# An attention and mixture-of-experts kernel: padding rows as indirect scatters, a drain behind them, and two subtractions on another engine

## The chip, the cores and the metric

The kernel runs on one core of a Trainium2 chip. The metric is device time in microseconds (us), the median of several runs. A core has five engines, each with an instruction stream of its own, which it works through in order: TensorE (PE: matrix products), VectorE (DVE), ScalarE (ACT), GpSimd (POOL) and SyncE (SP, which here only issues DMAs). They wait for each other, and for DMAs, through semaphores. Sixteen DMA engines move the data that SP and GpSimd ask for.

## The reference

First comes attention with random features: for each batch and head, `q` and `k` are projected on 128 random directions, exponentiated, and combined without a softmax over keys. Its output, one row of 512 values for each of 4608 tokens, is the input `x` of a mixture of 8 experts with one expert per token:

```
q_p, k_p = phi(q * scale), phi(k * scale)          # phi: projection on omega, exp
num = q_p @ (k_p^T v);  den = q_p . sum(k_p) + 1e-6
x = (num / den) as [4608, 512]

logits = normalized(x) @ normalized(expert_emb)^T / tau
expert_idx = argmax(logits, axis=1);  gate_w = softmax(logits)[expert_idx]
for e in range(8):
    mask = expert_idx == e
    h = maximum(x[mask] @ w1[e], 0)                # 512 -> 1024
    out[mask] = gate_w[mask] * (h @ w2[e])         # 1024 -> 512
```

## The kernel before

**First stage.** A loop works on 36 tiles of 128 tokens. For each tile it forms the features, the attention output and the logits; for each three tiles it chooses the experts and counts tokens (`routed`). GpSimd then writes each tile's 128 rows (512 values, 8 logits and the token's number: 521 floats) into a DRAM tensor `xs` with one indirect DMA (L592). There each expert has a region of 4736 rows, and a token's row is the region's start plus the number of its expert's tokens so far. Beside the last tiles TensorE already computes steps 0 and 1 of the second stage (`first_steps`).

**Second stage.** It has 38 steps of 128 rows of one expert each; step `t` begins with a load of 128 rows of `xs` on SP's queue (`xload`, L189). TensorE turns the rows (L269), multiplies with `w1`, and then with `w2` (L287). Every float32 value is split into a high and a low part, so each product takes three matmuls. The result is written to the rows of `y` that the token numbers name, by an indirect DMA of GpSimd (`store`, L317); a row whose number is too large is skipped.

**Weights.** Each step also loads a quarter of the `w1` and of the `w2` of an expert to come (`wload`, L205) and splits it (`wsplit`). For the first four quarters ScalarE makes the high part (L232), and VectorE (`w1`) or GpSimd (`w2`) subtracts it from the loaded value for the low part (L234).

**Padding.** The last step of an expert reads up to 127 rows behind its last token. These must hold a token number that `store` skips. So when all tiles are routed, 128 rows of padding are written behind each expert's last row, from `padrow`, an SBUF tile. The first row's place comes from `runi`, which VectorE computes (L985 to L989). `pad(0)`, for the expert of steps 0 to 2, is issued on SP. The seven others are ordinary DMAs of GpSimd (L993); GpSimd loads each place from `runi` into a register first (L992), and in front of all seven stands a drain (L998), at which GpSimd stops until its earlier work is done.

**What sets the order.** All engines are written out by hand here (`manual_schedule`): an engine's order is the order of the code. Waits come from what each instruction reads and writes, corrected by `declare_no_dep` and `add_manual_dep`. `xload` lets step 3 (`NPRE + 1`) go without the seven last paddings, while step 4 waits for all of them. The pools `p1`, `small` and `once` end with the first stage (`c1`, L325), and the pool `p2` (L1073) takes their memory; the `xs` rows of steps 3 and 4 (`xg`) lie in `p2`. GpSimd's DMAs use eight semaphores in turn, named DMASW0 to DMASW7.

Of the kernel before, what the change touches and what calls it, by code (L numbers as in the profile page):

```python
# [13 lines left out]
I32 = mybir.dt.int32  # L14
# [3 lines left out]
ALU = mybir.AluOpType  # L18
AX = mybir.AxisListType
ET = mybir.EngineType  # L20
PSUM = bass.MemoryType.PSUM

P = 128
B, H, S, D, M = 8, 8, 576, 64, 128
E, F = 8, 1024
# [7 lines left out]
GPICK = 5  # L33
DUM = E * REG
ROWS = DUM + P
RS = 576
PAY = DM + E + 1
NQ = 4
LAG = 7
NPRE = 2  # L40
# [1 line left out]
LOADS = {29: 0, 30: 2, 31: 1, 33: 4, 35: 6, 36: 3, 37: 5, 39: 7}  # L42
LOADS_LATE = 33
FILLS = {36: 1, 37: 1, 38: 1, 39: 1, 40: 1, 41: 1, 42: 2, 43: 4, 44: 5}
PADP = 8
ONACT = 3
DRAINS = (4,)
KPROJ = {0: (0,), 1: (1, 2), 2: (3,), 3: (4,), 4: (5,), 5: (6,)}
# [14 lines left out]
WHY = "computed on the chip from counts that sum to the token number"  # L63
# [3 lines left out]
def attention_moe(ctx: ExitStack, tc: tile.TileContext, qT, kT, v1, omT, emb, tau, w1q, w2q, xs, out):  # L67
    nc = tc.nc
# [39 lines left out]
    stepf = const.tile([P, 1], F32, name="stepf")  # L108
# [15 lines left out]
    runi = const.tile([P, E], I32, name="runi")  # L124
# [10 lines left out]
    put, got, outs, last_x, junks, kept = [], [], [], [], [], {}  # L135
# [4 lines left out]
    padrow = w1l[:, 1, 2, 0:PAY].bitcast(F32)  # L140
# [41 lines left out]
    def written(w):  # L182

        for o in put + got:
            tc.declare_no_dep(w.ins, o.ins.name, reason="other rows")
        put.append(w)

    def xload(t, row, xg):
        r = nc.sync.dma_start(xg, xs[ds(row, P), 0:PAY])  # L189
        if t in range(NPRE + 3):  # L190
            for j, w in enumerate(put):
                if t < NPRE and j > 3 * GPICK + 3 and w is not kept.get(t) or t == NPRE + 1 and j > len(put) - PADP:

                    tc.declare_no_dep(r.ins, w.ins.name, reason="other rows")
                else:
                    tc.add_manual_dep(r.ins, w.ins.name, sync, reason="rows written in any order")
        else:
            tc.add_manual_dep(r.ins, last_x[0].ins.name, sync, reason="behind an earlier step's wait")
        got.append(r)
        last_x[:] = [r]  # L200
        return xg
# [25 lines left out]
    def wsplit(wn, t, raw, dv, dp):  # L227
        _, h, l = W[wn]
        at = lambda a, d: a.rearrange("p a q f -> p (a q) f")[:, ds(d, 1), :].rearrange("p o f -> p (o f)")
        if t is not None and t < NQ:  # L230

            ih = nc.scalar.activation(h[:, 1, t, :], raw, AF.Copy)  # L232
            eng = nc.vector if wn == "w1" else nc.gpsimd
            ils = [eng.tensor_tensor(l[:, 1, t, :], raw, h[:, 1, t, :].bitcast(F32), op=ALU.subtract)]  # L234
        else:
            ih = nc.vector.tensor_copy(at(h, dv), raw)  # L236
            ils = []
            piece = F if t is None or t >= NSTAT - 2 else PIECE
            eng, d = (nc.vector, dv) if wn == "w2" and t is not None and t >= NSTAT - 2 else (nc.gpsimd, dp)
            for c in range(0, F, piece):  # L240
                c = slice(c, c + piece)
                ils.append(eng.tensor_tensor(at(l, d)[:, c], raw[:, c], at(h, d)[:, c].bitcast(F32), op=ALU.subtract))  # L242
        if t is None:
            return
        for w in (ih, *ils):
            seq[w] = len(seq)
            if t >= NQ:
                tc.add_manual_dep(w.ins, mmi[wn, t - 1][-1].ins.name, sync, reason="the buffer's last use")
        for o in range(NSTAT):
            apart(wn, (ih, *ils), t, mmi.get((wn, o), ()), o)  # L250
        if t < NPRE:

            for w in put:
                for il in ils:
                    tc.declare_no_dep(il.ins, w.ins.name, reason="another part of the weights")
        for w in spl.get((wn, t - 1), ())[1:]:
            tc.declare_no_dep(ih.ins, w.ins.name, reason="another part of the weights")
        spl[wn, t] = (ih, *ils)
# [3 lines left out]
    def flush():  # L262
        while lows:
            lows.pop(0)()
# [60 lines left out]
    with ExitStack() as c1:  # L325
# [453 lines left out]
        for i in range(NTILE + LAG + 2):  # L779
# [15 lines left out]
            if i == XLOAD:  # L795
                prow = [nc.values_load(
                    firsti[0:1, t : t + 1], engines=[ET.SP], min_val=t * P, max_val=(E - 1) * REG + t * P,
                    skip_runtime_bounds_check_because=WHY) for t in range(NPRE + 1)]
# [183 lines left out]
        vt = nc.vector  # L982
        t = lambda n, w=E, dt=F32: once.tile([P, w], dt, name=n)
# [3 lines left out]
        vt.tensor_copy(runi[:, 0:1], swp[:, 0:1])  # L987
        vt.tensor_scalar(swp[:, 1:2], run[:, 0:1], swp[:, 0:1], None, op0=ALU.subtract)
        vt.scalar_tensor_tensor(runi[:, 1:], isf[:, 1:], swp[:, 1:2], run[:, 1:], op0=ALU.mult, op1=ALU.add)  # L989
        def pad(e):  # L990
            eng, et = (nc.gpsimd, ET.Pool) if 0 < e < PADP else (nc.sync, ET.SP)
            v = nc.values_load(runi[0:1, e : e + 1], engines=[et], min_val=0, max_val=DUM - P, skip_runtime_bounds_check_because=WHY)  # L992
            written(eng.dma_start(xs[ds(v, P), 0:PAY], padrow))  # L993

        pad(0)
        xload(NPRE, prow[NPRE], xgp[NPRE])

        nc.gpsimd.drain()  # L998
        for e in range(1, PADP):
            pad(e)  # L1000


        row = lambda a: a.unsqueeze(1).to_broadcast([P, E, E])
# [52 lines left out]
        vt.tensor_scalar(r, tab[:, 1:2], -float(NQ), float(NQ), op0=ALU.mult, op1=ALU.add)  # L1056
        vt.tensor_tensor(tab[:, 3:4], r, q4, op=ALU.add)
        vt.tensor_copy(tab[:, 4:5], total)
        for _ in range(FILL2):
            next(fill, None)  # L1060
            flush()
# [88 lines left out]
    with tc.manual_schedule(engines={ET.PE, ET.Activation, ET.DVE, ET.Pool, ET.SP}):  # L1150
# [82 lines left out]
        for t in range(NPRE, NSTAT):  # L1233
# [11 lines left out]
            if early:  # L1245
                wn = joined(t - 1)
# [43 lines left out]
            if late and not early:  # L1290
                wn = words(t - 1), turn[t - 1][0].shape[1] * P
# [134 lines left out]
```

## Time and profile before

| what | value |
|---|---|
| median of 3 runs | 630.5 us (629.82 to 630.67) |
| the profiled execution | 630.09 us |
| its span, first to last instruction | 628.4 us |
| TensorE (PE) busy | 620.4 us, 99% |
| VectorE (DVE) busy | 496.5 us, 79% |
| ScalarE (ACT) busy | 432.5 us, 69% |
| GpSimd (POOL) busy | 421.2 us, 67% |
| mean granted TensorE clock | 0.998 of full speed |

The profiled execution took 1.7 us more than its span, for what lies around the first and the last instruction. Busy time is the time in which an engine had an instruction in work. Starts of instructions are counted from the start of the span. The name of a tile before an arrow is what is written, behind it what is read. A name at an idle time ("<-") is what ended last before the engine went on. The DMA rows of a queue give the time of the issue; the transfer lands later.

### The profile page before, as it was taken

The numbers are of one execution on the slowest core, as the hardware profiler recorded it, in microseconds if no ns is written. First come the engines' busy times: TensorE is split into PE (matmuls) and PEld (weight loads), VectorE is DVE, ScalarE is ACT, GpSimd is POOL, SyncE is SP. The second block draws the span as 40 slices with busy tenths as digits, with TensorE's granted clock in tenths as the row PEclk, the third lists the DMA queues.
The fourth block names the chain that finished last, engine by engine and source line by source line (L and its number), as shares of the span: only waits on it lengthen the run. The fifth ranks groups of instructions, "written<-read, shape, count | busy, mean of one in ns | idle before, by whom it ended". The sixth has DMA issues, their size and how long they took to land.

```text
span 628.4 us, 19172 instructions
## 1 busy us (share of the span) xinstructions
PE 620.4 (99%) x6337; PEld 531.1 (85%) x6338; DVE 496.5 (79%) x917; ACT 432.5 (69%) x1135; POOL 421.2 (67%) x603
## 2 busy tenths in 40 slices
PE   9999999999999999999999999999999999999996
PEld 8999999999988787888888888888888888888885
DVE  5799899898989836779787877887887886877764
ACT  6999899899888237675757566656666656575630
POOL 3013344456887534588898878896987989796862
PEclk9999999999999999999999999999999999999999
DMA  7754776777772487698787796867787775968731
GB/s 259 221 154 156 240 198 206 223 220 237 274 254 79 154 305 253 187 273 233 225 217 238 180 263 189 244 191 211 226 211 243 201 245 171 255 196 197 221 118 47
DMA packets 143263, 132.19 MB, mean 210 GB/s; under 512 B 107766, under 2 KB 107894, under 8 KB 143168
## 3 DMA queue, kind: packets, MB, share of 16 engines
q1 hardware_dynamic: 136544, 109.96, 60.7%
q0 software_dynamic: 6480, 20.91, 8.6%
q8 instruction: 57, 0.93, 0.6%
q14 instruction: 38, 0.31, 0.2%
q10 hardware_dynamic: 144, 0.07, 0.0%
HBM read 83.78 MB, written 21.97 MB: 168 GB/s over the span
## 4 chain that ended last, share of the span: by engine, by line
PE 89%; issue 3%; DVE 3%; POOL 1%; ACT 1%; DMA 1%; POOLq 1%; DVEq 0%; ACTq 0%
PE po L287 30%; PE pb L287 30%; PE pb L376 11%; PE kva L408 5%; PE nuu L485 5%; PE nuu L465 2%; PE fs_a L287 1%; PE nuu L408 1%; DMA raww<-w2q 1%; DVE nmq L380 1%; PE pb L94 1%; POOLq L992 0%; PE pb L435 0%; DMA qt<-qT 0%; POOL w2l L234 0%
## 5 line engine op out<-in xcount | busy, mean ns | idle before, releaser
L242 POOL TENSOR_TENSOR w2l<-raww,w2h 128x256 f32 x128 | 140.3, 1096 | 7.6
L242 POOL TENSOR_TENSOR w1l<-raww,w1h 128x256 f32 (+1 forms) x130 | 116.0, 892 | 14.5 <-DMA xgp<-xs 5.2
L287 PE MATMUL po<-w2h,hh 128*128 (+1 forms) x288 | 112.3, 390 | 0.0
L287 PE MATMUL po<-w2l,hh 128*128 (+1 forms) x288 | 112.1, 389 | 0.0
L287 PE MATMUL po<-w2h,hl 128*128 (+1 forms) x288 | 112.1, 389 | 0.0
L287 PE MATMUL pb<-w1h,xh 128*128 (+1 forms) x280 | 109.6, 391 | 0.3 <-ACT nuu L298 0.3
L287 PE MATMUL pb<-w1h,xl 128*128 (+1 forms) x280 | 109.2, 390 | 0.0
L287 PE MATMUL pb<-w1l,xh 128*128 (+1 forms) x280 | 109.0, 389 | 0.0
L1140 DVE COPY pl<-pb 128x512 uint16<-128x512 uint16 x68 | 46.8, 690 | 59.8 <-ACT pl L1136 59.1
L1136 ACT ACTIVATE pl<-pb 128x512 uint16<-128x512 uint16 x68 | 39.4, 582 | 67.9 <-PE pb L287 65.2
L390 ACT ACTIVATE ftq<-pb,nmq 128x128 f32<-128x128 f32 x288 | 80.1, 415 | 4.2 <-DVE nmq L380 4.2
L317 POOL DMA_INDIRECT y<-xgp,tail x36 | 44.6, 1239 | 54.0 <-DVE w1h L236 30.2
L390 ACT ACTIVATE ftk<-pb,nmk 128x128 f32<-128x128 f32 x272 | 75.9, 466 | 4.5 <-DVE nmk L380 4.5
L1158 DVE COPY wd<-t 128x1024 uint16<-128x1024 uint16 x68 | 65.1, 959 | 1.6 <-DMA t<-pl 1.5
L1174 ACT ACTIVATE hh<-wd 128x1024 fp32r<-128x1024 f32 x34 | 36.1, 1063 | 42.1 <-DVE wd L1158 37.1
L287 PEld LDWEIGHTS po<-w2h,hl 128*128 128x128 f32 x288 | 54.1, 188 | 11.4
L287 PEld LDWEIGHTS po<-w2h,hh 128*128 128x128 f32 x288 | 54.1, 188 | 11.1
L287 PEld LDWEIGHTS po<-w2l,hh 128*128 128x128 f32 x288 | 54.0, 187 | 11.1
L287 PEld LDWEIGHTS pb<-w1h,xh 128*128 128x128 f32 x280 | 52.5, 188 | 11.3 <-ACT w2h L232 0.7
L287 PEld LDWEIGHTS pb<-w1h,xl 128*128 128x128 f32 x280 | 52.5, 188 | 11.2 <-DVE xl L271 0.2
L287 PEld LDWEIGHTS pb<-w1l,xh 128*128 128x128 f32 x280 | 52.7, 188 | 10.8
L1178 DVE SCALAR_TENSOR_TENSOR hl<-wd,hh 128x1024 fp32r<-128x1024 f32 x34 | 54.7, 1610 | 2.9 <-ACT hh L1174 2.3
(351 smaller groups left out, 1250.0 us busy)
## 6 DMA issues: line engine op xcount, KB each, us to landing
raww<-w1q SPq DMA_DIRECT2D x38, 512.0 KB, 4.5
raww<-w2q SPq DMA_DIRECT2D x38, 512.0 KB, 4.8
qt<-qT SPq DMA_DIRECT2D x36, 256.0 KB, 3.1
kt<-kT SPq DMA_DIRECT2D x35, 256.0 KB, 3.6
xg<-xs SPq DMA_DIRECT2D x23, 260.5 KB, 2.8
xgp<-xs SPq DMA_DIRECT2D x15, 260.5 KB, 3.6
rf<-w1q SPq DMA_DIRECT2D x4, 512.0 KB
rf<-w2q SPq DMA_DIRECT2D x4, 512.0 KB, 3.9
```

The source lines that it names most:

```text
L242: ils.append(eng.tensor_tensor(at(l, d)[:, c], raw[:, c], at(h, d)[:, c].bitcast(F32), op=ALU.subtract))
L287: done.append(nc.tensor.matmul(dst, x[:, c * P : (c + 1) * P], ws.rearrange("p o f -> p (o f)"), start=(begin and i == 0 and k == 0), stop ...
L317: w = nc.gpsimd.indirect_dma_start(out=out, out_offset=bass.IndirectOffsetOnAxis(ap=(xg[:, DM:] if tail is None else tail)[:, E : E + 1].b ...
L376: nc.tensor.matmul(st["pj" + w, i, a][:, c, :], st[w, i][r, c, :], om[r, :], start=True, stop=True)
L390: nc.scalar.activation(ft[:, h, :], pj[:, h, :], AF.Exp, bias=nm[:, h : h + 1])
L408: nc.tensor.matmul(acc[c : c + 64, h, :], ft[:, h, c : c + 64], vt[:, 2 * h + a, :], start=begin and h == 0, stop=u == 4 + 4 * b and h == 3,)
L485: nc.tensor.matmul(pn[a][s * D : s * D + D, h, :], st["qp", i, s][:, 2 * h + a, :], kvs[sb, int(u > 4 - s)][:, 4 * a + h, :], start=True, ...
L1136: nc.scalar.activation(planes[1][:, o : o + 512], halved(src)[:, :, 1], AF.Copy)
L1140: nc.vector.tensor_copy(planes[0][:, o : o + 512], halved(src)[:, :, 0])
L1158: nc.vector.tensor_copy(to, src)
L1174: nc.scalar.activation(hh, wd[:, 0:F], AF.Relu)
L1178: nc.vector.scalar_tensor_tensor(hl, wd[:, 0:F], 0.0, hh.bitcast(F32), op0=ALU.max, op1=ALU.subtract)
```

## The change

The seven paddings become indirect scatters. VectorE computes a table `padi` of 128 rows by 8 experts: the row of `xs` for each of the 128 padding rows, or a row beyond the end of `xs` for those that lie past the expert's last step, and these the DMA skips. The table lies in the pool `once`. The scatters need no registers. They and the drain now stand behind the code of the step table, with the drain behind the scatters; on GpSimd itself nothing else lay between. In `wsplit`, the low parts of `w2`'s quarters 0 and 1 move from GpSimd to VectorE.

```diff
-PADP = 8
...
-                if t < NPRE and j > 3 * GPICK + 3 and w is not kept.get(t) or t == NPRE + 1 and j > len(put) - PADP:
+                if t < NPRE and j > 3 * GPICK + 3 and w is not kept.get(t) or t == NPRE + 1 and j > len(put) - E:
...
-            eng = nc.vector if wn == "w1" else nc.gpsimd
+            eng = nc.vector if wn == "w1" or t < NPRE else nc.gpsimd
...
-        def pad(e):
-            eng, et = (nc.gpsimd, ET.Pool) if 0 < e < PADP else (nc.sync, ET.SP)
-            v = nc.values_load(runi[0:1, e : e + 1], engines=[et], min_val=0, max_val=DUM - P, skip_runtime_bounds_check_because=WHY)
-            written(eng.dma_start(xs[ds(v, P), 0:PAY], padrow))
-
-        pad(0)
+        v = nc.values_load(runi[0:1, 0:1], engines=[ET.SP], min_val=0, max_val=DUM - P, skip_runtime_bounds_check_because=WHY)
+        written(nc.sync.dma_start(xs[ds(v, P), 0:PAY], padrow))
         xload(NPRE, prow[NPRE], xgp[NPRE])
-
-        nc.gpsimd.drain()
-        for e in range(1, PADP):
-            pad(e)
...
         vt.tensor_copy(tab[:, 4:5], total)
+
+        padi, over = t("padi", dt=I32), t("over")
+        vt.tensor_scalar(padi, runi, P - 1, None, op0=ALU.bitwise_and)
+        vt.tensor_scalar(over, padi, stepf, float(P), op0=ALU.add, op1=ALU.is_ge)
+        vt.scalar_tensor_tensor(over, over, float(ROWS), runi, op0=ALU.mult, op1=ALU.add)
+        vt.tensor_scalar(padi, over, stepf, None, op0=ALU.add)
+        for e in range(1, E):
+            written(nc.gpsimd.indirect_dma_start(
+                out=xs, out_offset=bass.IndirectOffsetOnAxis(ap=padi[:, e : e + 1], axis=0),
+                in_=padrow, in_offset=None, bounds_check=ROWS - 1, oob_is_err=False,
+            ))
+        nc.gpsimd.drain()
```

`PADP` and `E` are both 8, so the rule of `xload` reads as before.

**SP, from the load of step 3's rows on.** Names in brackets are the semaphores for which a row waits; `xg_5242` is the tile of step 3, `xg_5243` that of step 4, `raww_0` to `raww_3` are quarters of weights, and DMASW lanes are GpSimd's DMAs. Before:

```order
L189 DMA xg_5242<-xs 128x521 [waits DMAHW3_49,DMAHW1_49,DMAHW4_49,PE_49,Pool_49]
L205 ISA
L205 DMA raww_0_5314<-w2q 128x1024 [waits DMAHW2_49]
L205 ISA
L205 DMA raww_1_5316<-w1q 128x1024 [waits Activation_49]
L205 ISA
L205 DMA raww_1_5318<-w2q 128x1024 [waits DMAHW5_49]
L205 ISA
L205 DMA raww_2_5320<-w1q 128x1024 [waits DMAHW0_49,DVE_49]
L189 ISA
L189 DMA xg_5243<-xs 128x521 [waits DMASW5_49,DMASW4_49,DMASW6_49,DMASW2_49,DMASW7_49,DMASW1_49,DMASW0_49]
```

In the changed kernel, where step 3's tile is `xg_5241` and step 4's `xg_5242`:

```order
L188 DMA xg_5241<-xs 128x521 [waits DMASW5_49,DMASW6_49,DMASW4_49,DMASW7_49,DMASW2_49,DMAHW1_49,DMASW1_49,DMAHW3_49,DMASW0_49,DMAHW4_49,PE_49,Pool_49]
L204 ISA
L204 DMA raww_0_5313<-w2q 128x1024 [waits DMAHW2_49]
L204 ISA
L204 DMA raww_1_5315<-w1q 128x1024 [waits Activation_49]
L204 ISA
L204 DMA raww_1_5317<-w2q 128x1024 [waits DMAHW5_49]
L204 ISA
L204 DMA raww_2_5319<-w1q 128x1024 [waits DMAHW0_49,DVE_49]
L188 ISA
L188 DMA xg_5242<-xs 128x521
```

The wait for the seven lanes moved from step 4's load to step 3's, four weight loads earlier in the queue.

**GpSimd, from the last token scatter to the first paddings.** `w1l` is the memory of `padrow`; the drain is not among these rows, and it stood behind the first of them. Before:

```order
L592 DMA xs<-xr_4978,posi_5047 38016x576 [waits Pool_49]
L992 TENSOR_LOAD runi [waits DVE_49]
L993 ISA
L993 DMA xs<-w1l 128x521
L992 TENSOR_LOAD runi
L993 ISA
L993 DMA xs<-w1l 128x521 [waits DMASW5_49]
```

And the end of the same piece, before, with the stores of steps 0 and 1 and the subtractions of `w2`:

```order
L993 DMA xs<-w1l 128x521 [waits DMASW2_49]
L317 DMA y<-xgp_139 4608x512 [waits DMAHW4_49,DMASW3_49,DVE_49]
L317 DMA y<-xgp_140 4608x512 [waits DMASW4_49,DVE_49]
L234 TENSOR_TENSOR w2l<-raww_0_5314,w2h 128x1024 [waits DMAHW2_49,Activation_49]
L234 TENSOR_TENSOR w2l<-raww_1_5318,w2h 128x1024 [waits DMAHW4_49,Activation_49]
L234 TENSOR_TENSOR w2l<-raww_2_5327,w2h 128x1024 [waits DMAHW0_49,PE_49,Activation_49]
```

In the changed kernel the whole piece reads so; the drain stands ahead of the first store:

```order
L591 DMA xs<-xr_4978,posi_5047 38016x576 [waits Pool_49]
L1057 DMA xs<-w1l,padi 38016x576 [waits DVE_49]
L1057 DMA xs<-w1l,padi 38016x576 [waits DMASW5_49]
L1057 DMA xs<-w1l,padi 38016x576 [waits DMASW6_49]
L1057 DMA xs<-w1l,padi 38016x576 [waits DMASW7_49]
L1057 DMA xs<-w1l,padi 38016x576 [waits DMASW0_49]
L1057 DMA xs<-w1l,padi 38016x576 [waits DMASW1_49]
L1057 DMA xs<-w1l,padi 38016x576 [waits DMASW2_49]
L316 DMA y<-xgp_139 4608x512 [waits DMAHW4_49,DMASW3_49,DVE_49]
L316 DMA y<-xgp_140 4608x512 [waits DMASW4_49,DVE_49]
L233 TENSOR_TENSOR w2l<-raww_2_5326,w2h 128x1024 [waits DMAHW0_49,PE_49,Activation_49]
```

Seven register loads and the drain in front went, and two subtractions left GpSimd.

**VectorE, around step 2's hidden layer.** `hl` is the low part of step 2's hidden layer, `pl` a copy of step 3's. Before:

```order
L234 TENSOR_TENSOR w1l<-raww_1_5316,w1h 128x1024
L271 TENSOR_TENSOR hl_5369<-pb_74,hh_5368 128x512
L271 TENSOR_TENSOR hl_5369<-pb_71,hh_5368 128x512
L234 TENSOR_TENSOR w1l<-raww_2_5320,w1h 128x1024
L1140 COPY pl_0_5392<-pb_72 128x512
```

In the changed kernel:

```order
L233 TENSOR_TENSOR w1l<-raww_1_5315,w1h 128x1024
L270 TENSOR_TENSOR hl_5368<-pb_74,hh_5367 128x512
L270 TENSOR_TENSOR hl_5368<-pb_71,hh_5367 128x512
L233 TENSOR_TENSOR w2l<-raww_0_5313,w2h 128x1024
L233 TENSOR_TENSOR w2l<-raww_1_5317,w2h 128x1024
L233 TENSOR_TENSOR w1l<-raww_2_5319,w1h 128x1024
L1143 COPY pl_0_5391<-pb_72 128x512
```

The two subtractions stand between step 2's `hl` and the next quarter of `w1`.

## Rows read from the trace of the kernel before

**Rows 1.** Stretches: from:to, length, busy us (count) of each engine, clock, DMA share, GB/s
```profile
210.00:245.00 35.00, 34.87 (x175) 28.06 (x173) 20.82 (x72) 15.22 (x23) 16.45 (x20) 1.00 0.70 252
245.00:612.00 367.00, 366.81 (x1626) 303.67 (x1627) 287.52 (x384) 232.24 (x473) 300.34 (x293) 1.00 0.76 215
```

**Rows 2.** TensorE in order of time: start us, us, line, what; step 3's turns, a gap
```profile
229.28 0.60 PE L269 MATMUL pb<-ident,xg 128*128 128x128 f32 x4
...
245.19 0.47 PE L287 MATMUL pb<-w1h,xh 128*128 x1 [0.27 <-ACT nuu L298]
```

**Rows 3.** The chain that ended last, 236 to 246 us: start us, us, what
```profile
236.86 2.41 POOL w2l L234
...
239.29 4.19 DMA raww<-w2q
```

**Rows 4.** GpSimd in order of time: last token scatters, first and last padding, three stores
```profile
215.42 0.97 POOL L592 DMA_INDIRECT xs<-xr,posi  x1 [0.30 <-issue]
216.69 0.98 POOL L592 DMA_INDIRECT xs<-xr,posi  x1 [0.30 <-issue]
222.04 0.61 POOL L993 DMA_DIRECT2D xs<-w1l  x1 [4.37 <-DVE xgp L294]
...
229.14 0.54 POOL L993 DMA_DIRECT2D xs<-w1l  x1 [0.41 <-issue]
230.01 1.02 POOL L317 DMA_INDIRECT y<-xgp  x1 [0.33 <-issue]
231.34 1.00 POOL L317 DMA_INDIRECT y<-xgp  x1 [0.30 <-issue]
...
374.23 1.41 POOL L317 DMA_INDIRECT y<-xgp,tail  x1 [2.06 <-ACT ex L307]
```

**Rows 5.** DMA issues, 216.6 to 217.9 us (the last scatter): count, us to landing
```profile
xs<-xr,posi POOLq DMA_INDIRECT x1, 3.0
```

**Rows 6.** All loads of L189
```profile
DMA to landing us min/median/max: 2.8/3.0/4.1
```

**Rows 7.** SP's queue in order of time: loads for steps 3 and 4, weights between
```profile
223.37 0.33 SPq L189 DMA_DIRECT2D xg<-xs  x1
223.89 0.36 SPq L205 DMA_DIRECT2D raww<-w2q  x1
224.43 0.33 SPq L205 DMA_DIRECT2D raww<-w1q  x1
...
237.41 0.33 SPq L189 DMA_DIRECT2D xg<-xs  x1
```

**Rows 8.** DMA issues, 229.0 to 229.3 us (the last padding): count, size, us to landing
```profile
xs<-w1l POOLq DMA_DIRECT2D x1, 260.5 KB, 8.1
```

**Rows 9.** ScalarE in order of time: the split of `w1`'s quarter 1
```profile
233.80 1.06 ACT L232 ACTIVATE w1h<-raww 128x1024 fp32r<-128x1024 f32 x1 [0.55 <-DMA raww<-w1q]
```

**Rows 10.** VectorE in order of time: `runi`, the step table, step 2's `hl`, what follows
```profile
213.65 0.22 DVE L989 SCALAR_TENSOR_TENSOR runi<-isf,swp,run 128x7 int32<-128x7 f32 x1
...
217.78 0.16 DVE L1057 TENSOR_TENSOR tab<-five 128x1 f32<-128x1 f32 x1
...
236.04 1.28 DVE L271 TENSOR_TENSOR hl<-pb,hh 128x512 fp32r<-128x512 f32 x2
239.59 3.12 DVE L234 TENSOR_TENSOR w1l<-raww,w1h 128x1024 fp32r<-128x1024 f32 x1 [2.27 <-DMA xg<-xs]
...
243.83 1.21 DVE L234 TENSOR_TENSOR w1l<-raww,w1h 128x1024 fp32r<-128x1024 f32 x1
```

**Rows 11.** TensorE in order of time: the step table's turn, step 2's use of `hl`
```profile
219.13 0.27 PE L1063 MATMUL pb<-ident,tab 128*5 128x128 f32 x1
...
239.27 0.39 PE L287 MATMUL po<-w2h,hl 128*128 128x512 f32 x1
```

**Rows 12.** The end of the span in stretches, columns as in rows 1
```profile
623.00:624.00 1.00, 0.28 (x2) 0.00 (x0) 0.00 (x0) 0.63 (x1) 0.00 (x0) 1.00 0.00 0
...
626.50:628.40 1.90, 0.00 (x0) 0.00 (x0) 0.00 (x0) 0.00 (x0) 0.00 (x0) 0.50 0.09 22
```

## Prediction

> **What bounds the kernel now.** I read the table of stretches first. From 210 to 245 us TensorE is busy for 34.87 of 35.00 us, from 245 to 612 for 366.81 of 367.00, and its granted clock is 1.00 in both [rows 1]. So hardly anything can be won around the change, and whatever stops TensorE there is added to the end, since nothing behind it gives time back. TensorE's own rows come next: at 229.28 it turns step 3's rows, without an idle time before it, and its only gap in this piece is 0.27 us at 245.19 [rows 2]. The chain of waits leads from that gap back over ScalarE to a load of `w2` issued at 239.29, which waited for GpSimd's subtraction of quarter 0 [rows 3]. Last I read GpSimd and SP. On GpSimd the seven paddings are issued from 222.04 to 229.14, behind a stop of 4.37 us [rows 4]. The last of them landed 8.1 us after its issue, at 229.14 + 8.1 = 237.24 [rows 8], and SP could issue step 4's load only at 237.41 [rows 7]. Step 3's load did not wait for paddings: it went out at 223.37, 5.9 us before TensorE's turn of its rows.
>
> **The change, part by part.**
>
> *A new wait.* In the order of the changed SP queue, step 3's load waits for all seven lanes of the paddings, and step 4's no longer does. The rule in `xload` lets step 3 go, so this is another dependency: the scatters read `padi`, `padi` lies in the pool `once`, and step 3's tile is the first of `p2`, which takes the memory of `once`. Paddings that took their places from registers read nothing of that pool. So the load for which TensorE is next in want now stands behind the last padding. Behind it in SP's queue stand four loads of weights and step 4's rows.
>
> *When the last padding lands.* The last token scatter begins at 216.69; scatters follow each other by 216.69 - 215.42 = 1.27 us [rows 4]. Seven more are at 216.69 + 7 x 1.27 = 225.58 for the start of the last. `padi` doesn't hold them up: it is made from `runi`, written at 213.65, by four small operations that stand ahead of the table's last ones [rows 10]. The last token scatter landed 3.0 us after its issue, with little else in flight [rows 5]; that is the nearest case, as no weights can be loading by then except the quarter asked for before step 3's rows. Landing: 225.58 + 3.0 = 228.58. Rows that are skipped save bytes, and I allow nothing for them.
>
> The Trainium skill ("DMA: Bandwidth & Descriptors", Anatomy of one DMA) gives a GpSimd DMA some 2.0 us fixed and its bytes at 436 GB/s beside, so 2.6 us for 128 rows as an estimate. The row says 3.0; by the page's figure the stall below would be 0.4 us shorter, and the trace's value is the one I use.
>
> *When TensorE goes on.* SP took 237.41 - 237.24 = 0.17 us from the last landing to the issue, which gives 228.75 for step 3's load. Loads of this kind take 2.8 us at least, 3.0 in the median [rows 6]; nothing but the first store goes beside this one and it is ahead of the weights, so I take 2.8: it lands at 231.55. TensorE wants it at 229.28. **Stall: 2.27 us**, on the engine that sets the end.
>
> Bounds of that term. Low: the same issue times, a scatter faster than the one row, 2.7 us, and the load at 2.8: 1.97 us. High: stores follow each other by 231.34 - 230.01 = 1.33 us [rows 4], so the last scatter begins at 226.00; with the slowest load time, 4.1 us, for both transfers, the end is 226.00 + 4.1 + 0.17 + 4.1 = 234.37, a stall of 5.1 us. In between, 3.0 for the load and 4.1 for the scatter give 3.6. I take the value nearest to the rows without much traffic.
>
> *The two subtractions.* They leave GpSimd (2.41 us for one, [rows 3]) and cost VectorE 1.21 us each, the time of the same shape on it [rows 10]. They lie behind step 2's `hl`, which ends at 236.04 + 1.28 = 237.32, where VectorE then idled until 239.59, 2.27 us for 2.42 of work. The next subtraction took 3.12 us before, while GpSimd was at its own, against 1.21 at 243.83; so `pl` comes earlier, not later, by some 1.7 us, and all of this shifts with TensorE's stall besides. The subtraction that frees the buffer of quarter 2's load ends at 237.32 + 1.21 = 238.53 in place of 236.86 + 2.41 = 239.27 [rows 3], 0.7 us sooner. That closes the gap of **0.27 us**. If the shorter time on VectorE were not had, `pl` would be where it is now, 0.15 us late, and the gap would stay.
>
> *The four new operations* add at most 4 x 0.22 = 0.9 us to the step table, by the longest small row [rows 10]. The table was done at 217.94, TensorE turns it at 219.13 [rows 11]: 1.19 us of cover, so nothing. Without that cover TensorE would lose up to 0.9 us.
>
> *The drain* now begins at 225.58 + 0.97 = 226.55; behind it stand the two stores. Even with the whole 4.37 us that lay ahead of the first padding before, the first store goes at 230.92, against 230.01 [rows 4]. Its tile is loaded again behind step 4's load only, so nobody waits for it: nothing. The register loads that go were on GpSimd alone.
>
> Sum: 2.27 - 0.27 = 2.0 us. The profiled execution took 630.09 us, so it would take **632.1**; it lies 0.4 us under the median of 630.5, and in medians the forecast is **632.5 us**, 0.3% slower. A measurement of this kernel can tell about 0.2%, 1.26 us, from no change. By the bounds 1.97 and 3.6 less 0.27 the forecast's own range is 632.2 to 633.8.
>
> **The rivals.**
>
> *No stall (not slower).* GpSimd issues the scatters faster, since many of their rows are skipped. The tokens per expert that the reference gives (605, 0, 553, 121, 1152, 1704, 0, 473) leave 552 of the 896 rows to write. For no stall the load must be out by 229.28 - 2.8 = 226.48, the last padding landed by 226.31 and issued by 223.31: a pitch of 6.62 / 7 = 0.95 us in place of 1.27. Below that it decides. Against it: the store of step 13 skips 88 of its 128 rows (1704 is 13 x 128 + 40) and still took 1.41 us on GpSimd [rows 4]. Then only the gap goes: 630.5 - 0.3 = 630.2 us. A change that is faster by more than 0.2% isn't in TensorE's rows at all, whose idle time in the two stretches is 0.13 + 0.19 us.
>
> *A second stall.* The five loads behind step 3's all go out at once. Quarter 1 of `w1` was issued at 224.43 and ScalarE waited for it until 233.80, 9.37 us later [rows 7, 9]; ScalarE makes step 2's high part `hh` behind that. Issued now 1.06 us after step 3's load, as before, at 229.81, with the same 9.37 it lands at 239.18. Before, `hl` was done 3.52 us after ScalarE began (237.32 - 233.80), so 242.70 now; TensorE wants it at 239.27 + 2.27 = 241.54 [rows 11]. That is 1.16 us more: 633.7. Against it: the paddings that shared the DMA engines are gone by then.
>
> *TensorE's clock falls in the stall.* The granted clock is 1.00 before and through the change [rows 1]; the only fall in these rows is at the end, where TensorE's last product ends at 623.28 and the clock is 0.50 (1.2 of 2.4 GHz) from 626.50 on [rows 12]. At that level products take twice their time, so 5 us there cost 2.5 us: 632.5 + 2.5 = 635.0. Against it: after none of the short gaps before does the clock of a stretch fall. The Trainium skill ("TensorE: Matmul & The Clock Gate", Part 1) has the rule that an idle TensorE is put back to its lower clock; the trace agrees at its end, and no row here shows a stall like this one.
>
> **How the numbers follow.** Forecast 72% (632.5), no stall 10% (630.2), second stall 12% (633.7), clock 6% (635.0). Slower by over 0.2% holds the forecast, the second stall and the clock, less a little for a stall at its low end: 0.86. Within 0.2% holds the rest of the no-stall case and that little: 0.11. Faster, by something that no row shows: 0.03. The range goes from 631.3, below the low bound of the stall with the run-to-run spread of 0.4 and part of the way to no stall, to 634.2, which takes in 3.6 us and the second stall.
>
> **What would show it.** Right: an idle time of TensorE of 2 to 3 us before the turn of step 3's rows; SP's load of step 3 at about 228.8, ended by GpSimd's paddings; seven scatters from 217.96 to 225.6 at 1.27 us; step 4's load right behind the weights, with no wait; two `w2l` rows of 1.2 us on VectorE; no gap at step 4's first product; each later step at the same length as before. Wrong: step 3's load out by 226.5, a pitch of scatters under 1 us, or a TensorE that turns step 3's rows at 229.28 as before. A second idle time of TensorE before step 2's product with `hl`, or a granted clock under 1.00 behind the stall, would show the other rivals.

## The result, and the profile after

The changed kernel took 635.03 us in the median of six runs (631.70, 632.76, and four from 634.98 to 635.65), the kernel before 629.93 us: a ratio of 1.0066, 95% interval 1.0042 to 1.0090. It is slower, as forecast, and by 2.5 us more than forecast; the median lies 0.8 us above the range.

The execution that was profiled is the fastest of the six, 631.70 us with a span of 630.0. In it the forecast can be followed row by row. The line numbers have moved by one or a few: L188 are the loads of rows, L268 the turns, L1057 the paddings' scatters, L1067 the copy of the step table.

The stretches that answer to [rows 1], with the same columns:

```profile
210.00:245.00 35.00, 32.93 (x167) 26.55 (x166) 20.32 (x77) 13.76 (x21) 14.16 (x17) 1.00 0.68 233
245.00:612.00 367.00, 367.00 (x1626) 303.89 (x1625) 287.58 (x384) 233.21 (x473) 300.36 (x293) 1.00 0.76 215
```

TensorE is idle for 2.07 us ahead of 245 and for nothing behind it; its granted clock is 1.00 throughout. The gap of 0.27 us [rows 2] has gone. TensorE's rows (start us, us, line, what, idle time before) at the turns of steps 2 and 3:

```profile
223.33 0.60 PE L268 MATMUL pb<-ident,xgp 128*128 128x128 f32 x4
...
231.43 0.63 PE L268 MATMUL pb<-ident,xg 128*128 128x128 f32 x4 [2.02 <-DMA xg<-xs]
```

The chain that ended last (start us, us, what) leads from that turn to the last padding:

```profile
225.62 2.85 DMA xs<-w1l,padi
...
228.78 2.52 DMA xg<-xs
```

GpSimd's queue, which answers to [rows 4]: seven scatters at a pitch of 1.28 us, and the first store 0.65 us later than before.

```profile
216.68 0.97 POOL L591 DMA_INDIRECT xs<-xr,posi  x1 [0.30 <-issue]
217.96 0.97 POOL L1057 DMA_INDIRECT xs<-w1l,padi  x1 [0.31 <-DVE tab L1048]
...
225.62 0.97 POOL L1057 DMA_INDIRECT xs<-w1l,padi  x1 [0.30 <-issue]
230.66 0.97 POOL L316 DMA_INDIRECT y<-xgp  x1 [4.07 <-issue]
```

SP's queue, which answers to [rows 7]: step 3's load 5.41 us later than before, the weights behind it, and step 4's load without a wait.

```profile
228.78 0.33 SPq L188 DMA_DIRECT2D xg<-xs  x1
229.30 0.33 SPq L204 DMA_DIRECT2D raww<-w2q  x1
...
231.45 0.33 SPq L188 DMA_DIRECT2D xg<-xs  x1
```

VectorE, which answers to [rows 10]: the copy of the turned table 0.04 us behind its turn, as before, and the two moved subtractions in 2.35 us.

```profile
219.43 0.21 DVE L1067 CAST tabi<-pb 5x64 int32<-5x64 f32 x1
...
240.15 2.35 DVE L233 TENSOR_TENSOR w2l<-raww,w2h 128x1024 fp32r<-128x1024 f32 x2
```

So this execution does what the forecast says: a stall of 2.02 us less the gap, 1.6 us more than the profiled execution before. Four of six executions took 3.3 to 3.9 us beyond that, and these had no profile. What is on record of them is the mean granted clock of the whole execution: 0.995 to 0.997 in these four, 0.999 and 1.000 in the two shorter ones. The experiments look for those 3.3 us.

### The profile page after: what moved, and what is told of

Same layout as the page of the kernel before. It is cut to its first block, busy times and chain, and to the rows that moved or that the text cites. A ratio compares the mean times of both kernels' runs of the same rounds, so it can differ in the third digit from the quotient of the medians.

```text
span 630.0 us, 19158 instructions
## 1 busy us (share of the span) xinstructions
PE 619.5 (98%) x6337; PEld 530.6 (84%) x6338; DVE 495.4 (79%) x923; ACT 432.1 (69%) x1135; POOL 419.3 (67%) x601
## 4 chain that ended last, share of the span: by engine, by line
PE 88%; DVE 4%; ACT 3%; DMA 2%; issue 2%; POOL 1%; POOLq 0%; SPq 0%; ACTq 0%; DVEq 0%
PE po L286 31%; PE pb L286 31%; PE pb L375 9%; PE nuu L484 5%; PE kva L407 5%; PE nuu L464 2%; PE fs_a L286 1%; DMA xs<-xr,posi 1%; ACT ftq L389 1%; PE nuu L407 1%; ACT ftk L389 1%; DVE nmq L379 1%; POOL xs L1057 1%; PE pb L268 1%; PE pb L93 0%
## 5 line engine op out<-in xcount | busy, mean ns | idle before, releaser
L241 POOL TENSOR_TENSOR w2l<-raww,w2h 128x256 f32 x128 | 144.3, 1127 | 7.6
L241 POOL TENSOR_TENSOR w1l<-raww,w1h 128x256 f32 (+1 forms) x130 | 112.5, 865 | 14.3 <-DMA xgp<-xs 5.0
L1161 DVE COPY wd<-t 128x1024 uint16<-128x1024 uint16 x68 | 66.6, 981 | 1.3 <-DMA t<-pl 1.2
```

Source lines behind the costliest of these rows:

```text
L1161: nc.vector.tensor_copy(to, src)
```

## The experiments

They ran in three groups of four, on three chips. The kernel before took 632.64, 632.86 and 632.83 us there, 2.7 to 2.9 us more than in the first comparison, and the changed kernel was 4.8, 6.4 and 5.1 us above it, near the 5.1 of the first comparison. "Copy late" is the time from the end of the table's turn on TensorE to the start of its copy on VectorE, "stalls" are TensorE's idle times in front of the turns of steps 2 and 3; both from the one profile of each kernel.

| run | kernel | median us | above before | ratio, 95% interval | copy late us | stalls us |
|---|---|---|---|---|---|---|
| first | changed | 635.03 | 5.10 | 1.0066 (1.0042 to 1.0090) | 0.04 | 0, 2.02 |
| e1 | changed | 637.46 | 4.82 | 1.0084 (1.0071 to 1.0097) | 6.10 | 2.27, 0 |
| e5 | changed | 639.26 | 6.40 | 1.0093 (1.0068 to 1.0119) | 6.88 | 3.05, 0 |
| e12 | changed | 637.94 | 5.11 | 1.0084 (1.0068 to 1.0101) | 6.92 | 3.09, 0 |
| e2 | `padi` in constants | 642.03 | 9.39 | 1.0145 (1.0129 to 1.0161) | 6.11 | 2.29, 0 |
| e3 | scatters alone | 637.64 | 5.00 | 1.0088 (1.0073 to 1.0102) | 6.14 | 2.31, 0.20 |
| e4 | subtractions alone | 633.62 | 0.98 | 1.0013 (1.0003 to 1.0023) | 0.04 | 0, 0 |
| e6 | plain transfers | 633.64 | 0.78 | 1.0009 (1.0000 to 1.0019) | 0.55 | 0.68, 0 |
| e7 | three scatters | 635.72 | 2.86 | 1.0048 (1.0033 to 1.0063) | 3.72 | 0, 1.67 |
| e8 | no drain | 638.76 | 5.90 | 1.0096 (1.0081 to 1.0112) | 5.52 | 1.69, 0 |
| e9 | empty scatters | 641.36 | 8.53 | 1.0130 (1.0101 to 1.0160) | 9.28 | 5.45, 0.47 |
| e10 | all rows written | 637.77 | 4.94 | 1.0083 (1.0054 to 1.0112) | 4.78 | 0.95, 0.83 |
| e11 | drain in front | 639.59 | 6.76 | 1.0110 (1.0093 to 1.0127) | 0.32 | 0, 0 |

e3, e8 and e10 stop once more between these two turns, for 0.73, 1.21 and 2.12 us, at products that wait for VectorE's `w1h`.

**What the medians hold besides.** Not all of a difference lies behind the paddings. On one chip the table's turn begins at 224.01 us in e5 and at 221.78 in e6, and from there to the end of the span it is 413.7 and 410.1 us: of the 5.8 us between the two spans, 2.2 are lost ahead of the first padding. The largest piece is this: GpSimd issues its first token scatter 3.35 us later, VectorE waits until that has landed, and TensorE waits for VectorE. GpSimd's and TensorE's rows in e5, then GpSimd's in e6:

```profile
60.73 1.21 POOL L591 DMA_INDIRECT xs<-xr,posi  x1 [4.15 <-PE kva L407]
68.29 0.71 PE L464 MATMUL nuu<-ident,ftq 64*128 64x64 f32 x16 [1.40 <-DVE base L566]
```

```profile
57.38 1.24 POOL L591 DMA_INDIRECT xs<-xr,posi  x1 [0.66 <-PE nuu L464]
```

All nine profiles of kernels in which GpSimd issues no plain transfer have the late scatter (59.87 to 60.86), the changed kernel's first profile too; the five others have not (56.52 to 57.38). TensorE stops there for 0.70 us in the first profile, for 0.72 to 1.75 in e2, e5, e8, e10 and e11, and not in e1, e3 and e12. In the first profile the time was made up before the table's turn (219.12 us against 219.13). In the nine a load of instructions (the trace's DMA queue 14) begins at 57.8 to 58.8, in the five none does between 55 and 64; whether GpSimd waits for it was not tried. The prediction has no term for this stop, and where one of two kernels has it, their times do not compare the paddings alone.

**The changed kernel again (e1, e5, e12).** No edit. Expected of e1:

> The changed kernel itself once more, to see where its time over 632 us goes. Theory A: TensorE's stall of about 2 us in front of step 3 (2.02 in the profile of 631.7) costs 1.8 us in every run, and in most runs the granted clock then falls to 0.50 for some microseconds, which costs 3 more; expected are runs in two groups, near 632 with a mean clock of 0.999 to 1.000 and near 635 with 0.995 to 0.997, a median of 633 to 635, and, if the profile falls into the upper group, a stretch right behind the stall at a granted clock of 0.50 whose products take about twice as long. Theory B: the 3 us are a second wait (raww w1 of step 1, hl, or a late xg) that only some runs have; expected is a TensorE wait of 2 to 3 us more between 230 and 260 us at a clock of 1.00.

All five runs lay between 636.14 and 639.05, and the two whose mean clock was 1.000 were not the short ones (637.27 and 638.10). Neither theory fits alone: the clock does fall in this profile, but behind a stall that neither named, 2.27 us in front of step 2. Its cause was the same in the two controls, of which e5 expected

> The changed kernel once more, as the control of the three beside it. In its second profile the stall stood in front of step 2 (2.27 us), because the copy of the table's turn (tabi, on VectorE) ran 6.1 us behind the end of that turn on TensorE, in the first profile 0.03 us behind it. Theory S: where the seven indirect scatters of the paddings run back to back on GpSimd, TensorE's signals arrive late in most executions; expected is a median 2.5 to 5.5 us above before, and in a profile of a run over 634 us (or 3 us above before) a copy of tabi 3 to 7 us late. Theory W: only the wait of step 3's load costs; expected is 1.7 to 2.2 us above before.

and e12

> The changed kernel as the control of the three beside it. Theory S: where before takes 632 to 633 us, 4 to 6.5 us above before and a copy of tabi 3 to 7 us late; where before takes 630, as on the chip of the first comparison, executions of both kinds, near 632 with the copy of tabi on time and near 635 with it 3 us late or more. Theory W: 1.7 to 2.2 us above before, whatever the chip.

The profile of e12 shows it best. GpSimd's scatters are as they were:

```profile
220.36 0.97 POOL L591 DMA_INDIRECT xs<-xr,posi  x1 [0.30 <-issue]
221.64 0.97 POOL L1057 DMA_INDIRECT xs<-w1l,padi  x1 [0.30 <-DVE five L1047]
...
229.29 0.98 POOL L1057 DMA_INDIRECT xs<-w1l,padi  x1 [0.30 <-issue]
```

TensorE turns the hidden layer of the first steps, then the table, and goes through the products of `fs_o` beside them:

```profile
220.58 1.04 PE L268 MATMUL pb<-ident,hp 128*128 128x128 f32 x8
...
222.83 0.27 PE L1066 MATMUL pb<-ident,tab 128*5 128x128 f32 x1
...
224.09 0.39 PE L286 MATMUL fs_o<-w2h,w2l 128*128 128x512 f32 x1
...
226.81 0.39 PE L286 MATMUL fs_o<-w2h,w2l 128*128 128x512 f32 x1
230.29 0.66 PE L268 MATMUL pb<-ident,xgp 128*128 128x128 f32 x4 [3.09 <-DVE tabi L1067]
```

VectorE and ScalarE wait for these results. First VectorE, then ScalarE (the name behind an idle time is the event that the profile saw end it, "remote" one that it can't name; it is not always what the instruction reads):

```profile
224.19 0.69 DVE L270 TENSOR_TENSOR w2l<-pb,w2h 128x512 fp32r<-128x512 f32 x1 [1.64 <-ACT w2h L269]
230.02 0.21 DVE L1067 CAST tabi<-pb 5x64 int32<-5x64 f32 x1 [5.15 <-remote]
232.23 0.75 DVE L293 TENSOR_SCALAR xgp<-fs_o,totalp 128x512 f32<-128x512 f32 x1 [1.99 <-PE pb L268]
```

```profile
221.22 0.60 ACT L269 ACTIVATE w2h<-pb 128x512 fp32r<-128x512 f32 x1 [2.58 <-issue]
223.55 0.60 ACT L269 ACTIVATE w2h<-pb 128x512 fp32r<-128x512 f32 x1 [1.74 <-PE pb L1066]
232.39 0.60 ACT L269 ACTIVATE w1h<-pb 128x512 fp32r<-128x512 f32 x1 [8.23 <-PE pb L268]
```

What the reader is to see: the second half of the first turn ends at 221.62 and ScalarE takes it up at 223.55; the table's turn ends at 223.10 and its copy starts at 230.02, although VectorE is free; the first half of `fs_o` ends at 224.48 and VectorE takes it at 232.23. TensorE's products themselves are not slow, from the row at 224.09 to the one at 226.81 there are twelve steps of 0.227 us. And the turn of step 2, which ends at 230.95, after twelve more products of `fs_o`, is taken up at 232.39, 0.16 us behind the older result. Two results made 6.5 us apart cannot become known 0.16 us apart unless it is TensorE's signals that are held, and not its work. The trace also keeps the times at which TensorE's semaphore was raised: 223.53, 230.00, 232.20 and 232.36, each 0.02 to 0.03 us ahead of one of these four starts; in the kernel before it is raised 0.01 to 0.02 us behind the end of the product. A signal of ScalarE is on time here: it ends at 224.15, in the middle of the scatters, and VectorE goes on with its result at 224.19. TensorE's signals are held from about the first padding to 2 us behind the last.

The stall follows from the code: the turned table and step 2's turned rows share a bank of PSUM (`pb[3]`), so TensorE waits for the copy. The step table is also what SP needs for step 3's load, which went out at 233.81, 4.5 us behind the issue of the last padding; that one took 2.85 us to land in the first profile. So the paddings should have landed by then, and the stall that the forecast prices is swallowed by this one: step 3's turn waits for nothing. Behind the stall the clock falls. Stretches of e12, columns as in [rows 1]:

```profile
210.00:245.00 35.00, 31.09 (x178) 24.92 (x178) 17.10 (x77) 10.03 (x16) 16.17 (x19) 0.95 0.57 206
245.00:612.00 367.00, 367.00 (x1628) 303.84 (x1627) 291.25 (x389) 235.56 (x471) 294.84 (x287) 1.00 0.77 217
231.30:234.60 3.30, 3.30 (x9) 2.62 (x8) 1.44 (x2) 0.60 (x1) 0.55 (x1) 0.50 0.46 161
```

The sum: 35.00 - 31.09 = 3.91 us idle and 3.30 x 0.5 = 1.65 us for the half clock, less the 0.13 + 0.19 us that TensorE was idle in the same stretches before [rows 1], is 5.2 us; the medians differ by 5.1. That they agree so well is in part luck: 0.82 of the 3.91 us lie in front of a turn at 214.11, ahead of the first padding at 221.64, and the kernel before has no profile on this chip. Behind the first padding it is 3.09 + 1.65 = 4.7 us. Theory S, the held signals, holds here, though e5's 6.40 us lie above the 5.5 that I allowed; W, the wait of step 3's load alone, falls. No chip where the kernel before takes 630 us came up again, so what S expects there was not seen.

**`padi` in the constants (e2).**

```diff
+    padi = const.tile([P, E], I32, name="padi")
...
-        padi, over = t("padi", dt=I32), t("over")
+        over = t("over")
```

> The row numbers of the paddings (padi) lie in the pool of constants, not in the pool that is given back before step 3's tile is taken from the same memory; so step 3's load no longer waits for the paddings, and step 4's does. Theory A: the wait goes (stall under 0.1 us in front of step 3), the fall of the clock goes with it, and the 0.27 us gap at step 4 stays closed: 629.6 to 630.0 in every run, mean clock 0.998 to 1.000. Theory B (the paddings, the drain or the moved subtractions disturb something themselves): the time stays at 632 or more. Rival C: step 4's load, which now waits for the last padding (landing near 228.5), is late itself: a wait in front of step 4 and 630.5 to 632.

A and C missed. B's 632 or more is met, though B does not say why it should be 642. Step 3's load waited for no padding, and nothing was won: it went out at 232.32, behind the late table. The kernel then lost 3.4 us more between 260 and 400 us, which no other kernel but e11 does, and e11 has the same edit. The stretch in e2, then in e1:

```profile
260.00:400.00 140.00, 136.57 (x600) 111.16 (x599) 105.48 (x146) 85.38 (x177) 103.81 (x109) 1.00 0.81 206
```

```profile
260.00:400.00 140.00, 140.00 (x623) 115.86 (x623) 113.65 (x151) 90.19 (x184) 118.54 (x115) 1.00 0.79 218
```

The chain goes there through loads of rows, of up to 4.77 us, and transposes by DMA; in e1 it stays on TensorE. The edit puts every tile behind the constants 32 bytes further in each partition; whether that is why was not tried.

**Each edit alone (e3, e4).** e3 is the changed kernel with the old line for the subtractions, e4 the kernel before with the new one:

```diff
-            eng = nc.vector if wn == "w1" or t < NPRE else nc.gpsimd
+            eng = nc.vector if wn == "w1" else nc.gpsimd
```

> The change without its second edit: the subtractions of w2 of steps 0 and 1 stand on GpSimd again. Theory A: the stall in front of step 3 is the whole cost, and step 4's weights have 2 us more slack behind it, so that the place of the two subtractions matters no more: stall 2.0, times in the same two groups as the changed kernel (632 and 635). Theory B (the two subtractions on VectorE delay hl or the w1l of step 2 and cost the rest): under 631.5 in every run.

> The kernel before with the second edit alone: the subtractions of w2 of steps 0 and 1 on VectorE. Theory A: no stall in front of step 3, and the 0.27 us gap of step 4 closes because the tile of its weights comes free earlier: 0.3 us faster than before, 629.5 to 629.8. Theory B: VectorE's two subtractions of 2.35 us put hl or w1l late: 630.5 or more, 635 if the clock falls.

e3 is the changed kernel over again (637.64 us against 637.46, stall in front of step 2 and not of step 3, as in e1), so the scatters are the whole cost. e4 is not the 0.3 us gain that I expected but 0.2 to 1.5 us slower. Its gap in front of step 4 is longer than before, TensorE's row in e4:

```profile
247.30 0.47 PE L287 MATMUL pb<-w1h,xh 128*128 x1 [0.54 <-DVE w1l L234]
```

The subtraction named there waited for quarter 3 of `w1`, which ScalarE could split only at 244.84. In the changed kernel the stall hides this.

e4 has none of the seven scatters, and in it signals come late behind the tokens' scatters. TensorE, GpSimd and VectorE in one listing from e4, then VectorE's row for the same work in the kernel before:

```profile
204.01 1.25 PE L485 MATMUL nuu<-kvs,qp 128*64 128x73 f32 x32
...
204.98 0.99 POOL L592 DMA_INDIRECT xs<-xr,posi  x1 [0.16 <-DVE mx L548]
...
206.33 0.98 POOL L592 DMA_INDIRECT xs<-xr,posi  x1 [0.16 <-issue]
...
207.02 0.17 DVE L506 TENSOR_SCALAR rr<-nuu 128x8 f32<-128x8 f32 x1 [1.22 <-PE nuu L559]
```

```profile
204.45 0.15 DVE L506 TENSOR_SCALAR rr<-nuu 128x8 f32<-128x8 f32 x1
```

In e4 TensorE ends at 205.26 and VectorE, free since 205.80, begins at 207.02; in the kernel before it began as soon as it was free. This is not one row alone. Up to 215 us the traces tell of some 310 raises of TensorE's semaphore. In the two profiles of the first comparison one of them lies more than 0.15 us behind the end of its product (0.20 us, in the kernel before); in the twelve others, e4 and e6 among them, 39 to 52 do, or are missing from the record. The last token scatter began at 218.7 to 221.7 in these twelve, and at 216.7 in the two. So it may be these held signals that make the kernel before 2.8 us slower on those chips; that is argued, not shown, as the kernel before has no profile there.

**Plain transfers in the same place (e6), and three scatters (e7).**

```diff
-            written(nc.gpsimd.indirect_dma_start(...
+            v = nc.values_load(runi[0:1, e : e + 1], engines=[ET.Pool], ...
+            written(nc.gpsimd.dma_start(xs[ds(v, P), 0:PAY], padrow))
```

> The paddings at the changed kernel's place, with its moved subtractions and with the drain behind them, but as the plain transfers with a row number in a register that the kernel before has. Theory S (the indirect scatters hold TensorE's signals back): the copy of tabi runs within 0.2 us of its turn, no stall in front of steps 2 and 3 (runi lies in the constants, so step 3's load waits for no padding), and the time is that of before within 0.6 us either way. Rival D (any transfer issued by GpSimd at this place does it, or the drain behind them): a copy of tabi 3 us late or more, and 3 us or more above before. Theory W (the wait of step 3's load alone): the same time as theory S, so that the two are told apart by the copy of tabi in the control and not here.

> Only the paddings of experts 1 to 3 as indirect scatters, those of 4 to 7 as plain transfers behind them. Step 3's load waits for the three scatters, which end 5 us earlier than the seven. Theory S: TensorE's signals are late only up to the third scatter's end, some 4 us behind the first one's start, so that the copy of tabi is 1 to 3 us late, the stall in front of step 2 is under 0.5 us, and the time lies 0 to 1.5 us above before. Rival D: as with seven, 3 us or more above before.

In e6 the seven transfers run from 220.51 to 227.66 in the midst of the same products, with more bytes, and the copy follows VectorE's own work at once; step 2's turn waits 0.68 us for its rows. VectorE's row in e6:

```profile
222.60 0.20 DVE L1065 CAST tabi<-pb 5x64 int32<-5x64 f32 x1
```

The copy's 0.55 us comes from one late signal behind the last token scatter (TensorE's turn ends at 220.56, ScalarE takes it up at 221.35). The time is that of before within 0.8 us, a little outside the 0.6 that I allowed. e7, with three scatters first, is between: VectorE's row, then TensorE's.

```profile
225.74 0.21 DVE L1070 CAST tabi<-pb 5x64 int32<-5x64 f32 x1 [2.40 <-remote]
```

```profile
233.83 0.63 PE L268 MATMUL pb<-ident,xg 128*128 128x128 f32 x4 [1.67 <-DMA xg<-xs]
```

The copy is 3.72 us late and the time 2.86 us above before, both more than expected (1 to 3, and 0 to 1.5), and the copy is still in time for step 2; but the table's loads on SP are late with it, and step 3's rows come 1.67 us late. None, three and seven scatters give 0.8, 2.9 and 6.4 us on one chip, though 1.40 us of the last are the early stop in e5's profile, which e6 and e7 do not have. Rival D, any transfer by GpSimd, falls.

**No drain (e8).**

```diff
-        nc.gpsimd.drain()
```

> The changed kernel without the drain behind the paddings' scatters. Theory S: the drain has no part in it, the signals are late and the time is that of the control within 0.7 us. Rival D' (GpSimd's pending drain, which stands 10.7 to 10.9 us in its queue, holds the signals back): the copy of tabi runs within 0.2 us of its turn, and the time falls to at most 2.2 us above before, the wait of step 3's load.

5.90 us against the control's 6.40, and the copy 5.52 us late without a drain: the drain has no part in it.

**Issue, bytes or skipped rows (e9, e10).** In e9 the seven scatters skip every row, and plain transfers write the paddings behind them; in e10 no row is skipped.

```diff
e9
-        vt.scalar_tensor_tensor(over, over, float(ROWS), runi, op0=ALU.mult, op1=ALU.add)
+        vt.tensor_scalar(over, runi, float(ROWS), None, op0=ALU.add)
e10
+        vt.scalar_tensor_tensor(over, over, 0.0, runi, op0=ALU.mult, op1=ALU.add)
```

> Seven indirect scatters whose row numbers all lie past the last row, so that they write no row, at the place of the paddings' scatters; the paddings themselves follow as seven plain transfers. Theory S, read as the issue on GpSimd (the writing of the transfers' lists, not the bytes that move): the copy of tabi is 3 us late or more, as with the seven that write, and the time is 4 us or more above before. Rival T (the rows that move, or their landings, hold the signals back): the copy of tabi is within 0.5 us of its turn, and the time is at most 2.5 us above before, of which the wait of step 3's load for the scatters is up to 2.

> The seven indirect scatters write all 128 rows each (896 rows instead of 552; none is skipped). Theory S: nothing changes but the bytes, the copy of tabi is 3 us late or more, and the time is that of the control within 1 us. Rival K (the skipped rows make a scatter hold the signals longer): the copy of tabi is late by under 1.5 us, as behind the tokens' scatters, which skip no row, and the time is at least 2 us below the control.

Scatters that write nothing hold the signals as long as any. GpSimd's and VectorE's rows in e9:

```profile
222.90 0.98 POOL L1057 DMA_INDIRECT xs<-w1l,padi  x1 [0.30 <-DVE tab L1046]
...
230.59 0.98 POOL L1057 DMA_INDIRECT xs<-w1l,padi  x1 [0.30 <-issue]
```

```profile
233.40 0.21 DVE L1070 CAST tabi<-pb 5x64 int32<-5x64 f32 x1 [8.67 <-remote]
```

So it is the issue of an indirect scatter on GpSimd, not the moved rows. e10 costs 4.94 us against 5.11 of its control, and its copy is 4.78 us late, so the skipped rows aren't it either. Rivals T and K fall.

**The drain in front (e11).** `padi` in the constants, and the drain ahead of the scatters, which moves them 4.56 us behind the last token scatter.

```diff
+        nc.gpsimd.drain()
         for e in range(1, E):
             written(nc.gpsimd.indirect_dma_start(
...
-        nc.gpsimd.drain()
```

> The seven indirect scatters behind GpSimd's drain, where the kernel before has its plain transfers, some 4 us later, and padi in the constants, so that step 3's load waits for none of them. Theory S: the copy of tabi passes ahead of them on time, but the signals of step 2's turn and of the shared expert's second product, which fall between the scatters, come 2 to 7 us late; step 2's products wait for their weights' copies on ScalarE, and the time is 3 us or more above before. Rival P (only the place in front of the table's copy hurts): the time is that of before within 0.7 us.

The copy is on time, and the time is no better: 6.76 us above before, of which 3.3 are lost between 260 and 400 us as in e2. The held signals now hit step 3's turn, and not step 2's weights, where I had put them. TensorE's row and ScalarE's in e11:

```profile
232.97 0.60 PE L269 MATMUL pb<-ident,xg 128*128 128x128 f32 x4
```

```profile
235.32 0.60 ACT L270 ACTIVATE xh<-pb 128x512 fp32r<-128x512 f32 x1 [5.25 <-DMA xs<-w1l,padi]
```

The turn ends at 233.57, and ScalarE splits it 1.75 us later: the trace has it waiting for a signal of TensorE that arrives at 235.17. The DMA named in the row is not what it reads. So a place other than the table's copy is hit too, which is against rival P. Its time is not refuted: behind the scatters TensorE stops for 0.94 us only, and the rest of the 6.76 is the 3.3 us that came with `padi`, an early stop of 0.72 us, and differences that no row here explains.

e11 also shows that not every signal among such scatters is late, and that not only TensorE's are. ScalarE's row behind step 2's turn, which ends at 227.63 between the third and the fourth scatter, and a row of VectorE that waits for its own result of 221.44, behind the tokens' scatters:

```profile
227.67 0.60 ACT L270 ACTIVATE w1h<-pb 128x512 fp32r<-128x512 f32 x1 [4.90 <-PE pb L269]
```

```profile
222.12 0.16 DVE L1049 TENSOR_TENSOR tab<-five 128x1 f32<-128x1 f32 x1 [0.69 <-DVE five L1048]
```

## Why the prediction was right and where it was wrong

- *The new wait.* Right. Step 3's load waits for all seven paddings and goes out at 228.78 (forecast 228.75); step 4's waits no more.
- *When the last padding lands.* Right in the first profile: issued at 225.62 (225.58), landed after 2.85 us (3.0). The Trainium skill's figure ("DMA: Bandwidth & Descriptors", Anatomy of one DMA), an estimate of 2.6 us, is further from this row.
- *The stall.* 2.02 us against 2.27: the load took 2.52 us, not 2.8.
- *The gap and the subtractions.* The gap closed and VectorE took 1.18 us for each subtraction, as put. That the moved subtractions alone close it is wrong: e4 has a gap of 0.54 us. Beside the stall it did not matter.
- *The four new operations and the drain.* Nothing, as put (e8 for the drain).
- *The step that failed* is the price of the seven scatters. I gave them their time on GpSimd and their landing, and put "1.19 us of cover, so nothing" on the table beside them. That signals of TensorE come 5 to 7 us late beside them was in no term and in no rival; nor was the early stop at GpSimd's first scatter (up to 1.75 us). Behind the first padding the held signals and the clock cost 4.7 us in e12, where the wait that I priced is hidden behind them. The mechanism that I forecast showed alone in the one execution that was profiled at first.
- *The four longer executions of the first comparison* stay open. That they had held signals too is inferred from the equal cost of 5.1 us, since none of them has a trace, and the two profiles taken there show no held signals, behind the tokens' scatters either. What is on record is their clock. Among the fourteen profiles, those with a fall of the clock behind a stall have a mean of 0.994 to 0.997, all others 0.998 to 1.000; so with 0.995 to 0.997 the clock most likely fell in these four.
- *The clock.* I gave it 6%, with 635.0. It falls in the profiles of e1, e2, e5, e9 and e12, there behind the stall of the held signals; it is a part, 1.65 us in e12, and e3, without the fall, is no faster than e1. Whether it fell in the first comparison behind the stall that I priced, as this rival has it, or behind another is not known; so neither is whether 635.0 was more than chance. By its price in e12 it would be half of the 3.3 us.
- *No stall, and a second stall behind `hl`.* Neither came. The scatters kept a pitch of 1.28 us with many of their rows skipped.

No kernel here beats the one before; e6 comes nearest, and is 0 to 0.19% slower.

## What to carry to other kernels

When a row of indirect scatters is put beside an engine that sets the end, price what the others wait for from it in that time, and not only the scatters' own queue: here seven cheap issues off the critical path cost more than the wait that they brought. A plain transfer with its row number in a register did the same work without that. And a profile of the fastest execution can confirm every row of a theory and still not be the usual case; where the runs stand in two groups, a trace of the slower one is needed. Compare two traces from the start of the span: here up to 2.2 us of a difference lay ahead of the edited code.

## What the runs showed of the hardware

- While GpSimd issued indirect scatters back to back, signals of TensorE arrived up to 7 us late (9 us in e9), while its products kept their pitch of 0.23 us (e12). ScalarE's signal in their midst was on time in e12 (0.04 us), VectorE's was 0.69 us late once in e11. Behind plain transfers of GpSimd no such delay was seen (e6). The Trainium skill ("SBUF — State Buffer", Who interferes with whom) says of contention for SBUF that TensorE and ScalarE never wait on anyone; the pitch agrees, but the signals are late all the same, which the page does not treat.
- It was there in every profile on three chips where such scatters stood in a row, though not for every signal (e11), and absent from the first profile with the same scatters at the same pitch. Why is open.
- Skipping all 128 rows of a scatter does not shorten its issue: 0.98 us in e9 as elsewhere.
- The clock stayed at 1.00 behind a stall of 2.02 us in the first profile and one of 2.31 us in e3; it fell behind one of 2.27 us in e1 (a mean of 0.61 from 229.0 to 232.5), and was at 0.50 (1.2 of 2.4 GHz) for 3.3 us behind one of 3.09 us in e12, where products followed each other by 0.43 us in place of 0.23.
- GpSimd's first indirect scatter went out some 3 us later in the kernels without a plain transfer on GpSimd (59.87 to 60.86 us against 56.52 to 57.38).
